# Batch 0's second 256 tokens by seven half-size products, w_out's first quarter ahead of w_in's last, and a new order of all steps

## The chip, the cores and the metric

The kernel runs on one core of a Trainium2 chip. The metric is the device time of one execution in microseconds. The core's engines run side by side, each in the order of its own program: TensorE (PE: matrix products), VectorE (DVE), ScalarE (ACT) and GpSimd (POOL: elementwise work; POOL here also issues the loads), and SyncE (SP: stores and transposes by DMA). They wait for each other by semaphores only.

## The reference

Cross attention between tokens and a small state, per batch and head, then two matrix products with a PReLU between:

```python
scores = scale * np.matmul(x, state.transpose(0, 1, 3, 2))     # B, H, S, D = 8, 8, 512, 64; 32 states
a = np.exp(scores - scores.max(-1, keepdims=True))
a /= a.sum(-1, keepdims=True) + 1e-09
xread = np.matmul(a, state)                                    # 512 rows per batch
scores2 = scale * np.matmul(state, x.transpose(0, 1, 3, 2))    # its softmax is a2
sread = np.matmul(a2, x)                                       # 32 rows per batch
x = concatenate([xread, sread])                                # 4352 rows of 512, heads side by side
h = x @ w_in                                                   # 512 x 2048
g = np.maximum(h, 0.0) + alpha * np.minimum(h, 0.0)
out = g @ w_out                                                # 2048 x 512
```

## The kernel before

Products are in float16, sums in float32. The work is cut by batch: batches 0 to 7 are 512 token rows each; "batch 8" is the 256 state reads of all batches together. The function has one method for each step, and a table of tokens, `ORDER` (lines 17 to 136), says in which order the steps are called; that order is each engine's program order. A token has the step's name, its indices, the engine where there is a choice (a ScalarE, v VectorE, p GpSimd), and the PSUM bank or buffer. There are eight banks of 128x512 float32; a product into a bank waits until the last reader of the bank is done.

The steps that matter here:

- `lx`, `wi`, `wo` (lines 199 to 262): loads of a batch's x, of a quarter of w_in (512 hidden columns) and of a quarter of w_out (512 hidden rows). GpSimd issues them all, and they land in the order of issue.
- Attention weights of tokens: `sc` scores on TensorE, `sb` a 32x32 transpose on VectorE (L466), `smax` (VectorE, L476), `ssh` (GpSimd, L482), `sexp` (ScalarE, L488), `ssum` (VectorE, L492, L493), `snorm` (GpSimd, L496), `wb` the transpose back on VectorE (L504). After `wb` of a batch its weights, aT, are ready. For the states: `tm` (L514), `tms`, `te` (ScalarE, L519, L527), `tsum` (L537), a DMA transpose, `rd` state reads (L553), `rn` (L565).
- `m` (L590): the states of a batch times a quarter of w_in; `mo` (L603) casts the two halves from PSUM. So a hidden row comes from the weights and `m`, without xread.
- `F` (L620), for a batch and one of 16 blocks of 128 hidden columns: two products of 512 columns, needing `wb` and `mo`; `f` (L641) is half of one. `N` (ScalarE, L652) writes the negative part, `G` (VectorE, L656) the PReLU of it, called prelude below, which also frees the bank.
- The second product in full size, `S` (L675): for 128 tokens, two of 16 blocks at a time, 512 columns; `O` (L719) copies the sum out. Eight `S` for 128 tokens.
- The second product of 256 tokens in seven half-size products in place of eight. The 2x2 blocks are: two quarters of 128 tokens, two halves of the hidden rows, two halves of 256 output columns. `W` (L745) makes four sums of w_out blocks, once for all batches, in two parts each. `A` (L765) makes the four sums of hidden blocks, two parts each. `P` (L793) is one of the seven products, in two parts of four matrix products of 256 columns: 14 `P` for 256 tokens. `C` (L805) copies a partial result out of the bank that is still added to, four times, and `D` (L810) adds the other banks to three of them. `st` stores 128 rows.
- `Z` (L272): products of zeros, in units of 128 columns, on TensorE at the start.

The two methods that the change calls more often read so:

```python
def hidden_sum(b, i, s, f, e, k):
    qa, qb = quarters(b, i)
    ...
        1: (block(b, qb, f), block(b, qb, f + 2)),
        2: (hc.get((b, i, 1, f)), block(b, qa, f)),
        3: (block(b, qa, f), block(b, qb, f)),
        4: (block(b, qa, f + 2), hc.get((b, i, 2, f))),
```
```python
            rows = {
                ...
                5: lambda: hc[b, i, 1, hf][:, j, :],
            ...
            cols = {
                ...
                5: lambda: wc[1][:, jc, :],
```

The seven-product form is used for both halves of batches 1 to 7 and for batch 8. Batch 0 is done in full size: 32 `S`, four `O`.

Of the kernel before, what the change touches and what calls it, by code (L numbers as in the profile page):

```python
# [22 lines left out]
mo.2.0.a.1.2 mo.2.0.a.0 Z.4.5 xt.1.1.0.5 xt.1.0.0.5 xo2.1.0.v xt.1.1.1.6 xt.1.0.1.6 xo2.1.1.v
f.0.2.0.4 f.0.2.1 N.0.2.0 G.0.2 F.0.3.7 N.0.3.1 G.0.3 m.3.0.1.2 mo.3.0.a.1.3 mo.3.0.a.0 Z.5.4
m.0.1.0.3 mo.0.1.a.1.4 wo.3 mo.0.1.a.0 lx.2 sc.1.2.5.6 tm.1 f.0.0.0.4 f.0.0.1 N.0.0.2 sb.1 f.0.1.0.2
f.0.1.1 N.0.1.3 G.0.1 tms.1 m.4.0.7.1 mo.4.0.a.0.5 te.1.0 te.1.1 m.0.2.0.3 mo.0.2.v.0.6 m.1.1.7.2
mo.1.1.a.1.7 mo.4.0.a.1 mo.1.1.a.0 mo.0.2.v.1 smax.1 lx.3 ssh.p.1 W.1.0.p W.1.1.p G.0.0 F.0.5.0
F.0.7.5 m.1.3.6.3 mo.1.3.a.0.8 mo.1.3.v.1 F.0.4.2 N.0.4.0 G.0.4 N.0.7.1 G.0.7 N.0.5.3 F.0.10.1
F.0.6.7 tsum.0 F.0.8.6 N.0.8.2 G.0.8 G.0.5 m.0.3.4.3 N.0.10.0 G.0.10 mo.0.3.a.0.9 mo.0.3.a.1
S.0.1.0.2 S.0.1.1 S.0.2.0.5 S.0.2.1 m.2.1.6.4 mo.2.1.v.0.10 sexp.1 ssum.1 snorm.p.1 N.0.6.1 G.0.6  # L30
m.1.2.0.3 mo.1.2.a.1.11 mo.1.2.a.0 S.0.2.2 F.0.9.1 S.0.1.2 F.0.13.6 N.0.9.2 G.0.9 N.0.13.3 G.0.13
F.0.11.3 N.0.11.0 G.0.11 S.0.0.0.0 S.0.0.1 S.0.0.2 wb.1 F.0.15.7 F.0.12.1 S.0.1.3 N.0.15.1 G.0.15
F.0.14.6 N.0.14.2 G.0.14 S.0.2.3 S.0.1.4 S.0.0.3 N.0.12.3 G.0.12 mo.2.1.a.1 F.1.5.3 N.1.5.0 G.1.5
F.1.12.7 N.1.12.1 G.1.12 F.1.0.4 N.1.0.2 G.1.0 F.1.1.6 F.1.3.1 N.1.3.3 G.1.3 S.0.2.4 F.1.4.3 N.1.4.0
G.1.4 F.1.8.7 N.1.8.1 G.1.8 S.0.1.5 S.0.2.5 N.1.1.2 G.1.1 F.1.2.4 N.1.2.3 G.1.2 F.1.15.1 N.1.15.0
G.1.15 S.0.1.6 S.0.1.7 O.0.1.a.0 F.1.10.3 N.1.10.1 G.1.10 S.0.2.6 S.0.0.4 xd.2 sc.2.2.6.7 sb.2 tm.2
m.4.2.2.4 mo.4.2.a.0.12 smax.2 S.0.2.7 O.0.2.a.1 mo.4.2.a.1 S.0.3.0.1 F.1.9.3 N.1.9.2 G.1.9 tsum.1
F.1.11.2 N.1.11.3 G.1.11 W.0.0.p W.2.1.p W.0.1.p W.2.0.p W.3.1.p W.3.0.p A.1.0.3.0.p.0 A.1.1.3.0.p.1
tms.2 te.2.1 F.1.6.5 N.1.6.0 G.1.6 S.0.3.1 S.0.3.2 F.1.7.4 S.0.0.5 te.2.0 N.1.7.1 G.1.7 S.0.0.6
S.0.0.7 O.0.0.a.2 tt.0 tt.1 rd.0.3 rd.1.6 rn.1 A.1.1.1.0.v.0 A.1.0.3.1.v.0 m.2.3.7.2 mo.2.3.a.0.13  # L40
mo.2.3.a.1 xd.3 st.0.2 st.0.1 tt.2 S.0.3.3 F.1.13.5 ssh.p.2 sexp.2 N.1.13.2 m.3.1.0.4 mo.3.1.a.1.1
mo.3.1.a.0 A.1.1.2.0.p.0 rn.0 sc.3.2.6.7 tm.3 tms.3 lx.4 A.1.0.1.0.p.1 ssum.2 snorm.p.2 S.0.3.4
P.1.1.1.0.2 F.1.14.3 P.1.1.1.1 G.1.13 N.1.14.3 G.1.14 A.1.1.1.1.p.0 S.0.3.5 S.0.3.6 P.1.0.2.0.4
P.1.0.1.0.0 S.0.3.7 te.3.0 te.3.1 tt.3 sb.3 P.1.1.2.0.5 P.1.1.2.1 C.1.1.1.a.3 D.1.1.0 P.1.0.1.1
O.0.3.a.1 st.0.3 st.0.0 tsum.2 wb.2 m.2.2.3.1 mo.2.2.a.1.4 mo.2.2.a.0 m.3.2.6.7 mo.3.2.a.0.6 rd.2.5
lx.5 xd.4 A.1.1.2.1.p.0 P.1.0.2.1 mo.3.2.a.1 rt.0.1 rdo.0.a rn.2 smax.3 P.1.1.6.0 A.1.0.2.0.v.1
A.1.0.4.0.p.0 F.2.7.3 N.2.7.0 G.2.7 F.2.1.5 N.2.1.1 G.2.1 C.1.0.1.a.0 D.1.0.0 F.2.8.6 N.2.8.2 G.2.8
F.2.2.7 F.2.3.1 N.2.2.3 N.2.3.0 G.2.2 P.1.0.6.0 F.2.5.3 N.2.5.1 P.1.1.6.1 F.2.0.5 N.2.0.2 G.2.5
G.2.3 P.1.0.5.0.4 C.1.1.2.a F.2.11.6 N.2.11.3 G.2.11 G.2.0 A.1.0.1.1.p.1 P.1.0.5.1 F.2.9.7 P.1.1.7.0
F.2.10.3 N.2.10.1 xd.5 G.2.10 F.2.4.1 N.2.9.0 G.2.9 F.2.14.6 N.2.4.3 G.2.4 N.2.14.2 G.2.14  # L50
A.1.1.3.1.p.1 A.1.0.2.1.p.1 P.1.0.6.1 C.1.0.2.a P.1.1.7.1 ssh.p.3 sexp.3 ssum.3 P.1.1.5.0.5 F.2.13.3
rt.2.7 rdo.2.a P.1.0.7.0 C.1.1.3.a.1 P.1.0.7.1 C.1.0.3.a.2 D.1.0.1 F.2.12.1 N.2.12.1 F.2.6.6
P.1.1.5.1 G.2.12 N.2.6.0 F.2.15.7 N.2.15.3 A.1.0.4.1.p.0 G.2.6 G.2.15 N.2.13.2 G.2.13 P.1.0.4.0
P.1.0.4.1 A.2.0.1.0.p.1 C.1.0.4.a A.1.1.4.0.p.1 P.1.0.3.0 A.2.1.3.0.p.1 P.1.0.3.1 D.1.0.2 st.1.0
D.1.1.1 P.1.1.4.0 P.1.1.4.1 C.1.1.4.a st.1.3 tsum.3 rd.3.6 rn.3 sc.4.2.0.1 snorm.p.3 wb.3 m.3.3.7.3
m.4.1.4.2 mo.4.1.a.0.9 mo.3.3.a.1.0 mo.3.3.a.0 A.1.1.4.1.p.1 A.2.0.2.0.p.1 P.1.1.3.0 mo.4.1.a.1
A.2.1.1.0.v.0 A.2.0.4.0.v.0 P.2.0.1.0.6 P.2.0.1.1 P.2.0.2.0.4 C.2.0.1.a.0 F.3.5.3 N.3.5.1
A.2.0.1.1.v.1 A.2.0.2.1.p.1 F.3.1.7 N.3.1.0 tm.4 tms.4 P.2.0.6.0 P.2.0.2.1 D.2.0.0 G.3.5 F.3.3.2
# [804 lines left out]
```

## Time and profile before

| what | value |
|---|---|
| median of three runs | 208.69 us (207.89 to 210.45) |
| the profiled execution's own time | 207.22 us |
| its span, first to last instruction | 205.4 us |
| granted TensorE clock | 1.000 |
| TensorE idle before 25 us, and from 25 to 200 us | 4.6 us, 0.25 us |
| x of batch 1 lands | 14.3 us |

Every time in the profile is in microseconds from the span's start unless marked ns. A row of the timeline has start, length, engine, line, operation, output and inputs, the count of instructions merged in it, and in brackets the idle time before them with what ended it. Consecutive instructions of an engine overlap a little at their ends, so the length of a row over its count is closer to an instruction's price than the mean of one.

### The profile page before, as it was taken

The page shows a single profiled execution, that of the slowest core. Times are in us where ns is not written, and L with a number is a line of the kernel's source. Part 1 is how long each engine was busy: PE and PEld are TensorE (multiplying, and loading weights), DVE is VectorE, ACT ScalarE, POOL GpSimd, SP SyncE. Part 2 cuts the span into 40 slices and gives each one's busy share as a digit, 9 for nine tenths or more (in the row PEclk, how much of TensorE's full clock was granted, in tenths as well). Part 3 has the DMA queues.
Part 4 walks back from the last instruction along what each step waited for, and adds up shares of the span by engine and source line. Part 5 has one row for each costly group of instructions (what it writes and reads, how often), then busy time and mean ns, then how long its engine had stood idle before and what let it go on. Part 6 is the DMA issues. An engine that isn't in the chain of part 4 may idle for free.

```text
span 205.4 us, 5181 instructions
## 1 busy us (share of the span) xinstructions
PE 197.1 (96%) x2023; PEld 131.4 (64%) x2023; DVE 181.6 (88%) x321; ACT 145.2 (71%) x319; POOL 159.6 (78%) x136
## 2 busy tenths in 40 slices
PE   7887999999999999999999999999999999999993
PEld 2542344445757766766557776776778777788882
DVE  4799999999999989999899999989999699995841
ACT  2599997889897679899898878869666476411120
POOL 7575489999989979998998899987997988502220
PEclk9999999999999999999999999999999999999999
DMA  5999999995999342749990135022000220031124
GB/s 81 195 203 209 204 206 197 185 232 54 163 163 178 66 153 58 100 103 158 194 163 3 53 123 135 3 105 102 0 0 3 111 93 3 2 131 62 69 102 156
DMA packets 39257, 23.22 MB, mean 113 GB/s; under 512 B 22320, under 2 KB 35008, under 8 KB 39232
## 3 DMA queue, kind: packets, MB, share of 16 engines
q0 software_dynamic: 12704, 8.59, 29.3%
q1 hardware_dynamic: 26496, 14.29, 28.4%
q8 instruction: 16, 0.26, 0.6%
q14 instruction: 9, 0.07, 0.2%
q10 hardware_dynamic: 32, 0.01, 0.0%
HBM read 17.31 MB, written 8.91 MB: 128 GB/s over the span
## 4 chain that ended last, share of the span: by engine, by line
PE 85%; DVE 5%; DMA 5%; POOL 1%; ACT 1%; issue 1%; ACTq 0%; POOLq 0%
PE ps L793 44%; PE ps L620 24%; PE ps L675 7%; DMA xg<-in_x_dram 5%; PE ps L629 3%; PE ps L590 3%; DVE gt_all L656 3%; PE ps L553 1%; ACT neg_all L652 1%; PE ps L362 1%; DVE m_all L603 1%; POOL xg L218 1%; DVE ts L466 1%; DVE nb L514 1%; DVE mx L476 1%
## 5 line engine op out<-in xcount | busy, mean ns | idle before, releaser
L656 DVE SCALAR_TENSOR_TENSOR gt_all<-neg_all,oma_sb,ps 128x512 f16<-128x512 f32 x128 | 89.3, 738 | 3.0 <-ACT neg_all L652 2.7
L652 ACT ACTIVATE neg_all<-ps 128x512 f32<-128x512 f32 (+1 forms) x144 | 77.4, 598 | 20.0 <-PE ps L620 14.4
L620 PE MATMUL ps<-aT,m_all 128*128 128x512 f16 x250 | 66.4, 379 | 0.3 <-DVE m_all L603 0.2
L765 POOL TENSOR_TENSOR hc_all<-gt_all 128x512 f16<-128x512 f16 x43 | 49.2, 1160 | 11.4 <-DVE osb_all L810 8.7
L793 PEld LDWEIGHTS <-hc_all 128*128 128x128 f16 x480 | 46.3, 98 | 14.3 <-issue 1.1
L793 PE MATMUL ps<-wc,hc_all 128*128 128x256 f16 x360 | 47.7, 273 | 0.0
L793 PEld LDWEIGHTS <-gt_all 128*128 128x128 f16 x336 | 32.6, 98 | 8.3 <-issue 0.5
L805 ACT COPY osb_all<-ps 128x256 f32<-128x256 f32 x51 | 19.1, 383 | 25.7 <-PE ps L793 22.2
L620 PEld LDWEIGHTS <-m_all 128*128 128x128 f16 x250 | 24.0, 98 | 18.0 <-issue 2.2
L603 ACT CAST m_all<-ps 128x512 f16<-128x512 f32 x58 | 31.6, 621 | 4.3 <-PE ps L590 4.3
L765 POOL TENSOR_TENSOR hc_all<-gt_all,hc_all 128x512 f16<-128x512 f16 x22 | 25.4, 1164 | 6.3 <-DVE hc_all L765 6.1
L793 PE MATMUL ps<-w_out_sb,gt_all 128*128 128x256 f16 x224 | 29.7, 273 | 0.0
L765 POOL TENSOR_TENSOR hc_all<-hc_all,gt_all 128x512 f16<-128x512 f16 x21 | 24.3, 1164 | 3.9 <-DVE hc_all L765 3.6
L810 DVE TENSOR_TENSOR osb_all<-osb_all,ps 128x256 f32<-128x256 f32 x45 | 18.0, 413 | 7.6 <-PE ps L793 4.7
L496 POOL TENSOR_TENSOR an<-ts,r 128x1024 f16<-128x1024 f32 (+1 forms) x9 | 15.5, 1725 | 6.2 <-DVE r L493 4.0
L482 POOL TENSOR_TENSOR ts<-ts,mx 128x1024 f32<-128x1024 f32 x7 | 13.4, 1918 | 5.4 <-DVE mx L476 5.4
L675 PE MATMUL ps<-w_out_sb,gt_all 128*128 128x512 f16 x64 | 16.6, 380 | 0.1
L793 PE MATMUL ps<-w_out_sb,hc_all 128*128 128x256 f16 x120 | 16.5, 273 | 0.0
L793 PE MATMUL ps<-wc,gt_all 128*128 128x256 f16 x112 | 14.7, 273 | 0.0
L590 PE MATMUL ps<-w_in_sb,stT 64*32 64x512 f16 x256 | 11.8, 383 | 1.9 <-DMA w_in_sb<-in_moe_w_in_dram 0.9
L527 ACT ACTIVATE e<-ps,nb 128x512 f16<-128x512 f32 x16 | 11.1, 705 | 0.1
L675 PEld LDWEIGHTS <-gt_all 128*128 128x128 f16 x64 | 5.9, 98 | 7.2 <-issue 1.2
(78 smaller groups left out, 204.6 us busy)
## 6 DMA issues: line engine op xcount, KB each, us to landing
out_dram<-osb_all SPq DMA_DIRECT2D x33, 256.0 KB, 2.6
xg<-in_x_dram POOLq DMA_DIRECT2D x7, 512.0 KB, 9.1
w_in_sb<-in_moe_w_in_dram POOLq DMA_DIRECT2D x4, 512.0 KB, 12.0
w_out_sb<-in_moe_w_out_dram POOLq DMA_DIRECT2D x4, 512.0 KB, 13.6
xg<-in_x_dram POOLq DMA_DIRECT2D x2, 256.0 KB, 4.5
out_dram<-osb_all SPq DMA_DIRECT2D x2, 128.0 KB, 2.4
gs_all<-in_state_dram POOLq DMA_DIRECT2D x1, 192.0 KB, 6.8
st<-in_state_dram SPq DMA_DIRECT2D x1, 128.0 KB, 2.4
```

Of the source, the lines that this page charges most:

```text
L482: engine(e).tensor_tensor(ts, ts, over_blocks(cols(softmax_tile("mx", b), j, S // N)), ALU.subtract)
L496: engine(e).tensor_tensor(blocks(cols(softmax_tile("an", b), j, S)), blocks(cols(softmax_tile("ts", b), j, S)), over_blocks(cols(softmax_t ...
L590: nc.tensor.matmul(banks[N * k : N * (k + 1), (k0, k1)[g], :], st_head(b, 2 * k + g)[64 * g : 64 * g + 64, :], w_in_sb[64 * g : 64 * g + 6 ...
L603: copier(e)(ms[b, f][:, g, :], banks[:, live["mp", b, f][g], :])
L620: nc.tensor.matmul(h.rearrange("p (r t) -> p r t", r=2), ms[b, f][:, g, 128 * j : 128 * (j + 1)], weights(b, g), start=(g == 0), stop=(g = ...
L652: nc.scalar.activation(neg, h, RELU, bias=0.0, scale=-1.0)
L656: nc.vector.scalar_tensor_tensor(gts[b, f][:, j, :], negs.pop((b, jc)), oma_sb[:, jc : jc + 1], hs.pop((b, jc)), ALU.mult, ALU.add,)
L675: nc.tensor.matmul(outs[b, q], hidden(b, jc, q), w_out_sb[:, jc, :], start=(jc == 0), stop=(jc == n_jc - 1),)
L765: engine(e).tensor_tensor(t, x, y, ALU.add if s == 1 else ALU.subtract)
L793: nc.tensor.matmul(outs[b, i, bank], rows, cols, start=(p in (1, 2, 5) and jc == 0), stop=(jc == n_jc // 2 - 1), skip_group_check=True,)
L805: copier(e)(rows_at(b, q, k)[:, 256 * half : 256 * (half + 1)], outs[b, i, "x"])
L810: nc.vector.tensor_tensor(to, to, outs[b, i, bank], ALU.add)
```

## The change

Only the table `ORDER` differs; it has two lines more, so line numbers behind it are higher by two (L656 becomes L658). The methods are the same.

```diff
-lx0.0 lx0.1 id ni.v wi.0 oma lst stc Z.7.32 stt.2 sto.a lx.1 wi.1 dd.0.0.v wi.2 Z.7.3 xt.0.0.0.6
+lx0.0 lx0.1 id ni.v wi.0 stc Z.1.22 stt.3 lst sto.a dd.0.0.v oma lx.1 wi.1 Z.1.10 xt.0.0.0.2
```

- Tokens 256 to 511 of batch 0 (quarters 2 and 3): 16 `S` and two `O` go; 14 `P`, eight `A` (six on GpSimd, two on VectorE), four `C` and three `D` come. Tokens 0 to 255 stay in full size.
- The loads are issued in the order w_in 0, 1, 2, w_out 0, w_in 3, w_out 1, 3, 2 in place of w_in 0 to 3, w_out 0 to 3.
- One part of one weight sum (`W`) moves to VectorE. Over the whole kernel 13 more `A` stand on GpSimd and five fewer on VectorE; VectorE has four more `C`, three more `D` and two fewer `mo`. Units of zeros: 73 before, 47 now.
- All steps get new places and banks.

VectorE, from the copies of batch 1's transposed x (L348, now L350) to the state maximum of batch 1 (L476, now L478). L656/L658 is the prelude, L603/L605 the cast of `m`, L514 and L466 the reductions and transposes of the scores. Before:

```order
L348 COPY xT_336<-ps 128x4x256 x2
L656 SCALAR_TENSOR_TENSOR gt_all<-neg_all,oma_sb,ps 128x512 x2
L514 TENSOR_REDUCE nb_395<-ps 128x2
L466 STREAM_TRANSPOSE ts_400<-ps 128x1024
L656 SCALAR_TENSOR_TENSOR gt_all<-neg_all,oma_sb,ps 128x512
L603 CAST m_all<-ps 128x512 x2
L476 TENSOR_REDUCE mx_441<-ts_400 128x32
```

And now:

```order
L350 COPY xT_332<-ps 128x4x256 x2
L658 SCALAR_TENSOR_TENSOR gt_all<-neg_all,oma_sb,ps 128x512
L468 STREAM_TRANSPOSE ts_377<-ps 128x1024
L516 TENSOR_REDUCE nb_394<-ps 128x2
L478 TENSOR_REDUCE mx_404<-ts_377 128x32
```

Two preludes and two casts less stand ahead of the maximum.

VectorE again, from there to the transpose that ends batch 1's weights (L504, now L506). Before:

```order
L476 TENSOR_REDUCE mx_441<-ts_400 128x32
L656 SCALAR_TENSOR_TENSOR gt_all<-neg_all,oma_sb,ps 128x512
L603 CAST m_all<-ps 128x512
L656 SCALAR_TENSOR_TENSOR gt_all<-neg_all,oma_sb,ps 128x512 x2
L537 RECIPROCAL r_0_308<-r_0_308 128x2
L656 SCALAR_TENSOR_TENSOR gt_all<-neg_all,oma_sb,ps 128x512 x3
L603 CAST m_all<-ps 128x512
L492 TENSOR_REDUCE r_1_511<-ts_400 128x32
L493 RECIPROCAL r_1_511<-r_1_511 128x32
L656 SCALAR_TENSOR_TENSOR gt_all<-neg_all,oma_sb,ps 128x512 x4
L504 STREAM_TRANSPOSE aT_550<-an_514 128x1024
```

And now:

```order
L478 TENSOR_REDUCE mx_404<-ts_377 128x32
L658 SCALAR_TENSOR_TENSOR gt_all<-neg_all,oma_sb,ps 128x512 x2
L605 CAST m_all<-ps 128x512
L658 SCALAR_TENSOR_TENSOR gt_all<-neg_all,oma_sb,ps 128x512 x2
L494 TENSOR_REDUCE r_1_428<-ts_377 128x32
L495 RECIPROCAL r_1_428<-r_1_428 128x32
L605 CAST m_all<-ps 128x512 x2
L658 SCALAR_TENSOR_TENSOR gt_all<-neg_all,oma_sb,ps 128x512 x3
L506 STREAM_TRANSPOSE aT_492<-an_431 128x1024
```

Three preludes and a reciprocal (moved ahead of the copies of x) less, one cast more.

GpSimd, from the loads of w_in's later quarters to the row sums of batch 0 (L765, now L767; wc is a weight sum, L745, now L747; an the norm, ts the shift). Before:

```order
L253 DMA w_in_sb<-in_moe_w_in_dram 128x4x512 x3
L496 TENSOR_TENSOR an_298<-ts_240,r_0_242 128x512 x2
L259 DMA w_out_sb<-in_moe_w_out_dram 128x4x512 x4
L201 DMA xg_377<-in_x_dram 128x8x256
L201 DMA xg_443<-in_x_dram 128x8x256
L482 TENSOR_TENSOR ts_400<-ts_400,mx_441 128x1024
L745 TENSOR_TENSOR wc_446<-w_out_sb 128x1024 x2
L496 TENSOR_TENSOR an_514<-ts_400,r_1_511 128x1024
L745 TENSOR_TENSOR wc_676<-w_out_sb 128x1024
```

And now:

```order
L255 DMA w_in_sb<-in_moe_w_in_dram 128x4x512 x2
L261 DMA w_out_sb<-in_moe_w_out_dram 128x4x512
L498 TENSOR_TENSOR an_246<-ts_240,r_0_242 128x512 x2
L255 DMA w_in_sb<-in_moe_w_in_dram 128x4x512
L261 DMA w_out_sb<-in_moe_w_out_dram 128x4x512 x3
L203 DMA xg_344<-in_x_dram 128x8x256
L203 DMA xg_397<-in_x_dram 128x8x256
L484 TENSOR_TENSOR ts_377<-ts_377,mx_404 128x1024
L747 TENSOR_TENSOR wc_419<-w_out_sb 128x1024
L767 TENSOR_TENSOR hc_all<-gt_all 128x512
L498 TENSOR_TENSOR an_431<-ts_377,r_1_428 128x1024
L747 TENSOR_TENSOR wc_419<-w_out_sb 128x1024
```

Two loads have changed places, and row sums of batch 0 stand between the weight sums.

VectorE's steps between two such transposes (`wb`), counted from the order; what is not in the table is the same:

| stretch | | preludes | row sums `A` | sums `D` | weight sums | norms `rn` | state maxima | `tsum` |
|---|---|---|---|---|---|---|---|---|
| batch 1 to batch 3 | before | 35 | 3 | 5 | 0 | 4 | 2 | 3 |
| | now | 38 | 7 | 8 | 1 | 3 | 2 | 3 |
| batch 3 to batch 4 | before | 14 | 3 | 7 | 0 | 0 | 2 | 0 |
| | now | 15 | 2 | 6 | 0 | 2 | 1 | 1 |

TensorE's steps left from the first `F` of a batch on: of batch 3, 96 `F` and 180 `P` before, 96 and 181 now, with one `rd` more; of batch 4, 80 `F`, 149 `P` before, 81 and 153 now, with one `rd` less.

More of the change, by code (lines that the diff above doesn't have):

```diff
@@ L23 @@
[L23 to L58, printed above, removed]
@@ new lines @@
+P.6.0.7.1 C.6.0.3.v.3 G.7.6 P.8.0.1.0.6 P.8.0.1.1 P.6.0.4.0 C.8.0.1.v.2 A.8.0.1.0.p.0 P.8.0.5.0.3
+P.6.0.5.1 D.6.0.1 P.6.1.3.1 D.6.1.2 D.6.0.0 st.6.2 A.8.0.1.1.p.0 A.8.0.2.1.v.0 P.7.1.1.0.2
+A.7.0.1.0.v.1 A.8.0.2.0.p.0 P.7.1.1.1 P.6.0.3.0 A.7.1.1.0.v.0 A.7.0.2.0.v.1 P.8.0.6.0 P.6.0.4.1
+C.6.0.4.a st.6.1 F.7.12.4 N.7.12.1 P.8.0.5.1 P.8.0.6.1 A.6.0.4.1.v.0 G.7.12 A.8.0.4.0.v.1
+A.8.0.3.1.v.1 C.7.1.1.a.1 A.7.0.3.0.p.0 C.8.0.2.a A.8.0.3.0.p.1 A.7.0.3.1.p.0 P.7.0.5.0.0
+P.7.0.1.0.1 P.6.0.3.1 P.7.1.2.0.4 P.8.0.7.0 P.8.0.7.1 A.7.0.1.1.v.1 A.7.1.1.1.v.0 D.6.0.2
@@ L136 @@
+A.7.0.4.1.p.1 P.7.0.3.0 P.7.0.3.1 D.7.0.2 st.7.0 P.7.0.4.0 P.7.0.4.1 C.7.0.4.a sv.7.1.0
 """
```

193 lines of the change are left out of this document (112 added, 81 removed).

## The prediction

> **What bounds the kernel now.** I read the page's shares first, then its 40 slices, then busy time by stage, then the orders of time of Vector, Scalar and TensorE where stages meet, then the chain of waits.
>
> ```profile
> span 205.4 us, 5181 instructions
> PE 197.1 (96%) x2023; PEld 131.4 (64%) x2023; DVE 181.6 (88%) x321; ACT 145.2 (71%) x319; POOL 159.6 (78%) x136
> PE   7887999999999999999999999999999999999993
> DVE  4799999999999989999899999989999699995841
> ```
>
> TensorE is full from the fifth slice to the last, and Vector is nearly as full up to the thirty-third. The stages below are cut where Vector ends batch 0's and then batch 1's, 3's and 4's attention weights (first column start and end, then length, then busy time of each engine).
>
> ```profile
> 16.35:33.61 17.26, 15.66 (x142) 6.17 (x135) 17.07 (x26) 15.96 (x35) 11.53 (x8) 1.00 1.28 205
> 33.61:73.44 39.83, 39.83 (x454) 23.41 (x453) 39.16 (x64) 33.41 (x73) 38.33 (x28) 1.00 0.90 152
> 73.44:96.33 22.89, 22.89 (x223) 15.69 (x221) 22.22 (x34) 20.88 (x49) 21.26 (x18) 1.00 0.56 106
> 96.33:201.90 105.57, 105.40 (x1016) 79.60 (x1014) 91.52 (x175) 65.40 (x148) 76.78 (x65) 1.00 0.29 76
> ```
>
> Up to 33.61 us Vector is busy for 17.07 of 17.26 and TensorE is not: Vector sets the pace. Up to 73.44 both are full: TensorE 39.83, Vector 39.16 of 39.83. Only after 96.33 has Vector 14 us to spare. How tightly the two are coupled shows where a batch's weights end (L504 on Vector) and its first hidden product begins (L620 on TensorE):
>
> ```profile
> 15.07 1.29 DVE L348 COPY xT<-ps 128x1024 f16<-128x1024 f16 x2 [0.32 <-PE ps L340]
> ...
> 32.37 1.24 DVE L504 STREAM_TRANSPOSE aT<-an 128x1024 f16<-128x1024 f16 x1
> ...
> 72.20 1.24 DVE L504 STREAM_TRANSPOSE aT<-an 128x1024 f16<-128x1024 f16 x1
> ...
> 93.97 1.21 DVE L476 TENSOR_REDUCE mx<-ts 128x32 f32<-128x1024 f32 x1
> 95.10 1.24 DVE L504 STREAM_TRANSPOSE aT<-an 128x1024 f16<-128x1024 f16 x1
> ```
> ```profile
> 34.03 1.24 PE L620 MATMUL ps<-aT,m_all 128*128 128x512 f16 x5
> ...
> 73.99 1.03 PE L620 MATMUL ps<-aT,m_all 128*128 128x512 f16 x4
> ...
> 96.92 1.03 PE L620 MATMUL ps<-aT,m_all 128*128 128x512 f16 x4
> ```
>
> Batch 1's weights end at 33.61 and its products begin at 34.03; batch 3's at 73.44 and 73.99; batch 4's at 96.33 and 96.92. TensorE takes them just in time, so work added to Vector ahead of these points delays TensorE, and TensorE, whose order is fixed and which has no idle time later, can't win it back. The end is TensorE's last product at 201.9 and a fixed tail:
>
> ```profile
> 28.15 0.43 PE ps L620 x2
> 28.58 0.43 PE ps L675 x2
> ...
> 195.98 5.91 PE ps L793 x54
> ...
> 201.91 0.37 ACT osb_all L805
> ```
>
> **What the change removes on TensorE.** 16 steps S go, 32 products of 512 columns at 0.43/2 = 0.215 us: 6.9 us. 14 steps P come, 56 products of 256 columns at 5.91/54 = 0.109: 6.1. TensorE saves 0.8 us. The copies on Scalar (two of 512 columns against four of 256) stay about level. This saving counts only where TensorE sets the end.
>
> **What it adds ahead of 73.44 us.** The prices per instruction, Vector's first, then Scalar's, then GpSimd's:
>
> ```profile
> 20.75 1.28 DVE L603 CAST m_all<-ps 128x512 f16<-128x512 f32 x2
> ...
> 25.64 0.16 DVE L537 RECIPROCAL r<-r 128x2 f32<-128x2 f32 x1
> ...
> 29.83 2.62 DVE L656 SCALAR_TENSOR_TENSOR gt_all<-neg_all,oma_sb,ps 128x512 f16<-128x512 f32 x4
> ...
> 48.14 0.28 DVE L565 TENSOR_TENSOR sn<-ps,r 128x128 f16<-128x128 f32 x1
> 48.34 0.87 DVE L765 TENSOR_TENSOR hc_all<-gt_all 128x512 f16<-128x512 f16 x2
> ...
> 71.08 0.74 DVE L810 TENSOR_TENSOR osb_all<-osb_all,ps 128x256 f32<-128x256 f32 x2
> ```
> ```profile
> 14.07 0.24 ACT L527 ACTIVATION_READ_ACCUMULATOR e<-ps,nb 128x1 f32 x1
> ...
> 20.30 0.75 ACT L527 ACTIVATE e<-ps,nb 128x512 f16<-128x512 f32 x1
> ...
> 21.64 2.10 ACT L603 CAST m_all<-ps 128x512 f16<-128x512 f32 x4
> 23.54 2.65 ACT L652 ACTIVATE neg_all<-ps 128x512 f32<-128x512 f32 x5
> ...
> 26.88 1.23 ACT L488 ACTIVATE ts<-ts 128x1024 f32<-128x1024 f32 x1
> ```
> ```profile
> L765 POOL TENSOR_TENSOR hc_all<-gt_all x43: 1146/1157/1272, 44.4 to 188.5; 128x512 f16<-128x512 f16 x43
> ...
> L745 POOL TENSOR_TENSOR wc<-w_out_sb x4: 2118/2130/2143, 25.1 to 36.1; 128x1024 f16<-128x1024 f16 x4
> ```
>
> First stretch, from xT of batch 1 (ready at 16.36, since x of batch 1 is loaded in the same place) to batch 1's weights. Vector now has five preludes of L656 fewer ahead of them (5 x 0.655 = 3.3), one cast fewer (0.64), one small reciprocal fewer (0.16): 4.1 us less, so by Vector alone the weights end at 33.6 - 4.1 = 29.5. But Scalar must pass 13 casts and 8 negatives at 0.53, two exponentials (20.30 to 21.64, 1.34), a shift (about 0.25) and the state exponential (26.88 to 27.84 where the next begins, 0.96) between the end of batch 0's exponentials (14.31) and the negative that the last prelude needs: 13.7 us. Also the second token shift now stands behind the product on w_in's first quarter, which puts its exponential about 0.6 later (an estimate: it ran while Scalar waited for that product). That is 28.6, then a prelude and the transpose, 1.9: 30.5. Scalar's bound is the later, so I take 30.4, 3.2 earlier than now; the two sums, 29.5 and 31.0 with a wait between, are the ends.
>
> Second stretch, from batch 1's weights to batch 3's. By the counts in the table Vector gets three preludes (2.0), four row sums of L765 (4 x 0.435 = 1.7), three sums of L810 (1.1) and one weight sum of twice a row sum's width, which Vector has never done here: between one row sum, 0.4, and what GpSimd needs for it, 2.1; nearest is two row sums, 0.9. One normalising goes (-0.3). Together 5.4 us: 39.83 + 5.4 = 45.2, and batch 3's weights end at 30.4 + 45.2 = 75.6 instead of 73.44. Vector's 0.67 us of idle time may swallow some of it; the long weight sum may add 1.2.
>
> From there TensorE. Batch 3's first product comes 0.55 later, at 76.15 instead of 73.99: 2.2 late. What is left for TensorE then is one P (0.44) and one step of state reads (32 small products, 0.3 as an estimate, less than a P) more than before: 2.9 in all. The same sum at batch 4: Vector's stretch loses 0.6 (one prelude and the normalisings more, one maximum and two sums fewer), so its product begins at 75.6 + 22.3 + 0.6 = 98.5 against 96.92, 1.6 late, with 1.9 more left (one F, four P, less a read): 3.5 at most, and 2.2 if the 0.67 idle in each stretch is used. I take **2.8 us slower**, with 1.0 and 4.5 as ends.
>
> The last rows of TensorE's order are of the same kind as before, so the tail is kept. The profiled run is 207.22 us for a span of 205.4, hence 210.0 as such; it lies 1.47 below the median of 208.69. Median predicted: 208.69 + 2.8 = **211.5 us**.
>
> **What I cost at nothing.**
>
> ```profile
> 13.45 3.04 POOL L259 DMA_DIRECT2D w_out_sb<-in_moe_w_out_dram  x4
> ...
> 23.24 1.91 POOL L482 TENSOR_TENSOR ts<-ts,mx 128x1024 f32<-128x1024 f32 x1 [5.00 <-DVE mx L476]
> 25.12 4.21 POOL L745 TENSOR_TENSOR wc<-w_out_sb 128x1024 f16<-128x1024 f16 x2
> ```
> ```profile
> w_out_sb<-in_moe_w_out_dram POOLq DMA_DIRECT2D x1, 512.0 KB, 11.0
> ```
>
> The exchange of two loads: w_out's first quarter was issued at 13.45 and landed 11.0 later, at 24.45. It takes w_in's place about 2 us earlier, and w_in's last quarter gets the 24.45. Its first product now stands behind a cast of Scalar that lies five steps ahead of the 28.6 above, near 26.0, which covers the landing. All other loads behind keep their slots. On GpSimd the issues move past nothing long.
>
> The eight new row sums, six on GpSimd: the state maximum now stands behind two preludes and two casts fewer (2.6), so it ends near 20.6 and the state shift near 22.6. From there to the sum that P.0.1.5.1 needs GpSimd passes seven weight sums (14.9), four row sums (4.6) and a norm (1.9): 44.0. TensorE's first product of batch 1 waits for the bank of the second prelude behind the transpose, 31.9, and P.0.1.5.1 lies 13.1 us of products behind that, near 45. So it is covered by 1 us; each us beyond is one lost.
>
> **A rule against the change.** The longest row sum of Vector beside a GpSimd sum took 0.54 (the pair at 48.34 took 0.87 together), and GpSimd's longest 1.27 against 1.16. The Trainium skill, SBUF — State Buffer, § SBUF: two separate sides, says that a Vector instruction with two SBUF inputs and a GpSimd one exclude each other for the whole instruction. By it the weight sum on Vector would wait out up to 2.1 us and each Vector row sum up to 1.2; the rows show about 0.1, so I leave it out of the sum.
>
> **Rivals.**
> 1. Not slower: Vector isn't the bound. If batch 1's weights end by 28 or Vector's added sums fall in gaps, TensorE's 0.8 us shows: 207.9. For it: TensorE is 96% busy, Vector 88% over the whole. Against it: 17.07 of 17.26 and 39.16 of 39.83.
> 2. Slower by far: GpSimd's row sums come late for P.0.1.5.1. W of w_out's third quarter waits for the load issued last; if GpSimd ends 2.6 us later than 44.0, the 1.0 of cover is gone and 1.6 come on top: 213.1, and over 2% from 2.3 us on.
> 3. A cold TensorE. The first fillers (below) took 0.45 each, 0.215 later; the change drops 26 of 73 units of filler, most between 11.9 and 17 us. If TensorE falls back there, some 3.4 us of products take double: 1.7 more, 213.2. Against it: it still gets real work at least every 2 us there. The Trainium skill, TensorE: Matmul & The Clock Gate, § Part 1, puts the fall behind a whole window of idleness of about 3.4 us; no row shows a fall.
> 4. The lock of SBUF, as a mechanism: one Vector weight sum held 2.1 and two row sums 1.2 each: 4.5 more at worst, 2.1 in the mean, 213.6.
>
> ```profile
> 1.32 3.60 PE L272 MATMUL ps<-gs_all 128*128 128x512 f16 x8 [1.32 <-DVE gs_all L266]
> ```
>
> **How the numbers follow.** Slower by 1.0 to 4.5 around 211.5: 0.53. Rival 1: 0.22; rival 2: 0.13; rivals 3 and 4: 0.04 each; faster than any of them: 0.04. About 2%, or 4.2 us, is what a measurement of this kernel can tell from no change: below 204.5 or above 212.9. Faster: 0.03. Slower: of the first case 0.07, of rival 2 0.10, of 3 and 4 0.05: 0.22. Within: 0.75. The range leaves out half of rival 1 below and the far half of rival 2 above: 208.1 to 214.0.
>
> **What would show it.** Batch 1's transposed weights ending near 30.4, batch 3's near 75.6, with Vector idle for under 1 us between; TensorE idle for some tenths at a time between 30 and 75, waiting for copies and preludes, and full after 98. It would be wrong if batch 3's weights end by 73.5, or if TensorE waits for GpSimd near 45, or for w_in at 24.5.

## The result, and the profile after

| | before | changed |
|---|---|---|
| median of 4 executions | 208.64 us (207.89 to 210.45) | 211.21 us (210.09 to 212.00) |
| ratio to before | | 1.0139 [1.0095, 1.0184] |
| profiled execution, its span | 207.22 us, 205.4 us | 210.09 us, 208.1 us |

The changed kernel is slower by 2.6 us, 1.4%; the interval of its ratio lies above 1, but 1.4% is inside the 2% that count as no difference here. A ratio leaves out executions more than 1.5% above the fastest of their kernel, a median takes all. The forecast was 211.5 us, 2.8 slower. The number came out; the sum behind it did not, as the views show one by one.

First the page of the changed kernel: its span, its shares and the slices of TensorE.

```profile
span 208.1 us, 5223 instructions
PE 196.4 (94%) x2039; PEld 132.8 (64%) x2039; DVE 181.8 (87%) x322; ACT 145.6 (70%) x319; POOL 171.9 (83%) x148
PE   7867899999999999999999999999999999999981
```

TensorE is busy for 0.7 us less than before, and the span is 2.7 us longer: 3.4 us more of idleness. That 0.7 is not the forecast's 0.8: the products of zeros alone are busy for 4.7 us in place of 6.8 (13 products in place of 21), so the rest of TensorE's work is not less by this view. The last digit but one tells where some of it lies: 8, where the row of before had a 9. Next the same four stages as in the prediction, cut anew where batch 1's, 3's and 4's weights end (start and end, length, busy time of each engine, clock, DMA).

```profile
16.36:29.53 13.17, 10.91 (x105) 3.87 (x104) 13.13 (x19) 13.17 (x29) 10.94 (x8) 1.00 1.23 203
29.53:73.58 44.05, 43.99 (x470) 26.81 (x469) 43.70 (x73) 37.08 (x80) 41.33 (x31) 1.00 0.87 143
73.58:95.96 22.38, 22.38 (x277) 15.44 (x277) 21.60 (x35) 19.98 (x46) 20.65 (x18) 1.00 0.58 119
95.96:203.60 107.64, 106.96 (x1000) 80.75 (x997) 92.51 (x172) 65.00 (x146) 87.42 (x75) 1.00 0.29 76
```

The first stage is 4.1 us shorter, the second 4.2 longer, the third 0.5 shorter, the last 2.1 longer. In the last one TensorE, which had 0.17 us of idleness in 105.57 before, has 0.68 in 107.64. The two ends of the second stage in the order of time of Vector, and where batch 3's and batch 4's products begin on TensorE:

```profile
28.29 1.24 DVE L506 STREAM_TRANSPOSE aT<-an 128x1024 f16<-128x1024 f16 x1
...
72.36 1.22 DVE L506 STREAM_TRANSPOSE aT<-an 128x1024 f16<-128x1024 f16 x1
```
```profile
74.36 0.59 PE L622 MATMUL ps<-aT,m_all 128*128 128x512 f16 x2
...
96.25 1.03 PE L622 MATMUL ps<-aT,m_all 128*128 128x512 f16 x4
```

Batch 3's weights end at 73.58 (before 73.44, forecast 75.6); its first product starts at 74.36 (before 73.99, forecast 76.15). So TensorE begins batch 3 only 0.37 us late, with the 0.7 us of added steps still ahead of it: 1.1 of the span's 2.7. Batch 4 says the same: its first product starts at 96.25, 0.7 earlier than before (96.92, forecast 98.5), with the forecast's 1.9 us more of steps ahead of it, 1.2 in all. In between Vector and TensorE are close to a tie. The chain of waits of the changed kernel runs through Vector's preludes up to 45 us and through TensorE's products from 46.6 on; before, it was TensorE's alone there.

```profile
29.53 13.21 DVE gt_all L658 x20
...
47.04 0.98 PE ps L795 x8
```

The rest is at the end. The chain of waits there, with start and length of each piece:

```profile
196.55 0.43 DVE osb_all L812
...
197.00 3.75 DMA out_dram<-osb_all
...
200.85 0.38 ACT osb_all L807
...
201.25 0.43 DVE osb_all L812
...
201.72 1.92 PE ps L795 x16
...
203.67 0.37 ACT osb_all L807
```

Before, this chain was TensorE alone to 201.9. Now a store stands in it. Batch 8's finished rows leave row buffer 2 from 197.00 on; the copy C.7.0.3.a.2 on Scalar needs that buffer, starts at 200.85, and behind it stand the sum D.7.0.1 on Vector and then P.7.0.3.0, which waits for the bank. TensorE's own row gives its idle time in the brackets. SyncE's rows of the changed kernel and of the kernel before show what follows: the stores of the last rows (L724 and L722 whole rows, L728 and L726 half rows).

```profile
201.72 1.03 PE L795 MATMUL ps<-w_out_sb,hc_all 128*128 128x256 f16 x8 [0.63 <-DVE osb_all L812]
```
```profile
202.13 1.45 SPq L724 DMA_DIRECT2D out_dram<-osb_all  x3
204.07 0.33 SPq L728 DMA_DIRECT2D out_dram<-osb_all  x1
```
```profile
200.62 1.20 SPq L722 DMA_DIRECT2D out_dram<-osb_all  x2
202.31 0.33 SPq L726 DMA_DIRECT2D out_dram<-osb_all  x1
```

From the issue of the last half row to the end of the span it takes 208.1 - 204.07 = 4.0 us; before it was 205.4 - 202.31 = 3.1. Three whole rows stand close ahead of it now, where there were two. The profiled executions of the runs below mostly bear this out: with three whole rows issued in some 1.45 us the tail is 3.8 to 4.0 us in four traces, with three in 1.86 us it is 3.3, and with two in 1.0 to 1.2 us it is 3.1 to 3.2. Two traces with the stores further apart do not fit, at 3.5 and 3.7 us. So the trace puts 0.6 us of waiting and 0.9 of tail on the end, 1.5 together, which the forecast had at nothing.

### The profile page after: what moved, and what is told of

Read it like the earlier page. It is cut to its first block, busy times and chain, and to the rows that moved or that the text cites. A ratio compares the mean times of both kernels' runs of the same rounds, so it can differ in the third digit from the quotient of the medians.

```text
span 208.1 us, 5223 instructions
## 1 busy us (share of the span) xinstructions
PE 196.4 (94%) x2039; PEld 132.8 (64%) x2039; DVE 181.8 (87%) x322; ACT 145.6 (70%) x319; POOL 171.9 (83%) x148
## 3 DMA queue, kind: packets, MB, share of 16 engines
q0 software_dynamic: 12704, 8.59, 28.6%
## 4 chain that ended last, share of the span: by engine, by line
PE 73%; DVE 14%; DMA 6%; POOL 1%; issue 1%; ACT 1%; ACTq 0%; POOLq 0%
PE ps L795 44%; PE ps L622 20%; DVE gt_all L658 9%; DMA xg<-in_x_dram 5%; PE ps L631 3%; PE ps L592 3%; DMA out_dram<-osb_all 2%; PE ps L555 1%; DVE ts L468 1%; DVE m_all L605 1%; ACT e L529 1%; DVE xT L350 1%; PE ps L364 1%; POOL xg L220 1%; DVE nb L516 1%
## 5 line engine op out<-in xcount | busy, mean ns | idle before, releaser
L658 DVE SCALAR_TENSOR_TENSOR gt_all<-neg_all,oma_sb,ps 128x512 f16<-128x512 f32 x128 | 88.7, 739 | 4.7 <-ACT neg_all L654 4.3
L767 POOL TENSOR_TENSOR hc_all<-gt_all 128x512 f16<-128x512 f16 x50 | 57.2, 1158 | 6.9 <-PE ps L795 6.4
L795 PEld LDWEIGHTS <-hc_all 128*128 128x128 f16 x512 | 49.4, 98 | 15.1 <-issue 2.5
L795 PE MATMUL ps<-wc,hc_all 128*128 128x256 f16 x384 | 50.5, 273 | 0.0
L795 PEld LDWEIGHTS <-gt_all 128*128 128x128 f16 x360 | 34.6, 98 | 9.4 <-issue 1.5
L605 ACT CAST m_all<-ps 128x512 f16<-128x512 f32 x60 | 33.0, 610 | 3.3 <-PE ps L592 3.3
L767 POOL TENSOR_TENSOR hc_all<-gt_all,hc_all 128x512 f16<-128x512 f16 x26 | 30.0, 1166 | 3.2 <-DVE hc_all L767 2.3
L795 PE MATMUL ps<-w_out_sb,gt_all 128*128 128x256 f16 x240 | 32.5, 273 | 0.0
L767 POOL TENSOR_TENSOR hc_all<-hc_all,gt_all 128x512 f16<-128x512 f16 x21 | 24.2, 1158 | 6.6 <-DVE hc_all L767 6.4
L795 PE MATMUL ps<-w_out_sb,hc_all 128*128 128x256 f16 x128 | 18.1, 273 | 0.6 <-DVE osb_all L812 0.6
L592 PEld LDWEIGHTS <-stT 64*32 64x32 f16 x256 | 3.8, 89 | 11.3 <-issue 7.4
L516 DVE TENSOR_REDUCE nb<-ps 128x2 f32<-128x1024 f32 x8 | 9.6, 1204 | 0.7 <-PE ps L364 0.6
```

What stands on the lines that cost most here:

```text
L592: nc.tensor.matmul(banks[N * k : N * (k + 1), (k0, k1)[g], :], st_head(b, 2 * k + g)[64 * g : 64 * g + 64, :], w_in_sb[64 * g : 64 * g + 6 ...
L605: copier(e)(ms[b, f][:, g, :], banks[:, live["mp", b, f][g], :])
L658: nc.vector.scalar_tensor_tensor(gts[b, f][:, j, :], negs.pop((b, jc)), oma_sb[:, jc : jc + 1], hs.pop((b, jc)), ALU.mult, ALU.add,)
L767: engine(e).tensor_tensor(t, x, y, ALU.add if s == 1 else ALU.subtract)
L795: nc.tensor.matmul(outs[b, i, bank], rows, cols, start=(p in (1, 2, 5) and jc == 0), stop=(jc == n_jc // 2 - 1), skip_group_check=True,)
```

## The experiments

Each comparison gives the ratio to the kernel before, run beside it on the same chip. The kernel before had 60 executions in all there, in three sets with medians of 208.19, 208.14 and 208.15 us. Since one rival is a cold TensorE, the granted clock that each execution shows is told where it matters; an execution "whose clock did not fall" is one with a mean of 0.995 or more.

### The end: a fifth row buffer

The one copy that waits goes to another buffer, a slot of the negatives that nothing reads any more.

```diff
     def rows_at(b, q, i):
         if i is not None:
-            osbs[b, q] = osb_all[:, i]
+            osbs[b, q] = osb_all[:, i] if i < 4 else neg_all[:, 2]
...
-C.7.0.3.a.2
+C.7.0.3.a.4
```

> The changed kernel with one edit: the output rows of tokens 128 to 255 of batch 7 go to a fifth row buffer (a slot of neg_all that nothing reads any more), so that their copy at 200.85 us need not wait 4.96 us for the store of batch 8's rows. Theory E (what the prediction left at nothing: some 1.6 us of the loss lie in the last 12 us, 0.7 as TensorE waiting behind that copy and 0.95 as a longer tail of the last store): TensorE's last product ends 0.6 to 0.8 us earlier, the whole comes 0.7 us (if the three whole-row stores still stand bunched before the last one) to 1.6 us earlier, 209.6 to 210.5 us. Theory V (the prediction's: Vector's added steps between batch 1's and batch 3's weights cost it all, the end is kept): 211.2 us, no change over 0.3.

Measured: 211.07 us, ratio 1.0111 [1.0058, 1.0164]. By the medians alone this is unclear. The profiled execution shows the mechanism itself: TensorE passes the place without a pause.

```profile
200.61 1.03 PE L790 MATMUL ps<-wc,gt_all 128*128 128x256 f16 x8
201.48 1.91 PE L790 MATMUL ps<-w_out_sb,hc_all 128*128 128x256 f16 x16
```
```profile
202.34 1.86 SPq L719 DMA_DIRECT2D out_dram<-osb_all  x3
204.69 0.33 SPq L723 DMA_DIRECT2D out_dram<-neg_all  x1
```

Its span is 208.0 with the last half row issued at 204.69, a tail of 3.3 us. But five of its six executions had a granted clock of 0.974 to 0.991; the one at 1.000 took 208.68 us. The fifth buffer in the kernel before is the control:

```diff
-            osbs[b, q] = osb_all[:, i]
+            osbs[b, q] = osb_all[:, i] if i < 4 else neg_all[:, 1]
...
-C.7.0.1.a.2
+C.7.0.1.a.4
```

> The kernel before with a fifth row buffer for the one copy that waits for a store there (1.67 us, at 190.85 us, while TensorE goes on). Both theories: 208.6 us within 0.3, since TensorE does not stand behind that copy; it is the control to the first run, and would show whether a fifth buffer by itself changes the time.

Measured: 209.09 us, 1.0027 [0.9996, 1.0057], no gain: a buffer is worth something only where TensorE stands behind the copy.

### The clock: zero products put back

```diff
-m.4.0.4.1
+Z.4.8 m.4.0.4.1
...
-F.0.3.2
+F.0.3.2 Z.1.4
```

> The changed kernel with 12 units of zero products put back where TensorE waits early on: 8 ahead of the product that waits for the states' copies (11.4 to 13.2 us in its trace), 4 ahead of the one that waits for w_in (18.3 to 19.3 us). Theory C (cold): in the runs of the changed kernel above their best the granted clock falls to 0.5 for some 3 us near 23.6 us, as the profile of the run with the fifth buffer shows (0.81, 0.50, 0.84 in 22 to 28 us after TensorE was busy 2.0 of 4 us); so mean clocks come to 0.996 or more, from 0.987 to 0.992, and the time to 209.6 to 210.3 us, from 211.2. Against it (places and end alone): clocks and time stay, 211.2 us within 0.4.

Measured: 210.21 us, 1.0093 [1.0059, 1.0127], five of eight executions at 0.998 to 1.000 and three at 0.992. The same with the fifth buffer:

```diff
-            osbs[b, q] = osb_all[:, i]
+            osbs[b, q] = osb_all[:, i] if i < 4 else neg_all[:, 2]
...
-m.4.0.4.1
+Z.4.8 m.4.0.4.1
...
-F.0.3.2
+F.0.3.2 Z.1.4
...
-C.7.0.3.a.2
+C.7.0.3.a.4
```

> Both repairs of the changed kernel: the 12 units of zero products and the fifth row buffer. If cold stretches and the end are the whole loss: 208.3 to 209.0 us, the kernel before within 0.4%. If Vector's added steps cost some 2 us of their own, as the prediction had it: 210 us or more.

Measured: 209.65 us, 1.0044 [1.0016, 1.0072], seven of twelve executions at 0.996 to 1.000. Between these two stands one edit, the buffer. By executions whose clock did not fall it takes 210.10 us without the buffer (median of five) and 208.62 with it (of seven), 1.5 us. Two of those seven, at 209.89 and 210.04 us, do not show it; by the ratios, and by the executions whose clock did fall (211.15 and 210.14), it is 1.0. So the end is worth 1.0 to 1.5 us, where the trace said 1.5.

The changed kernel once more, unaltered:

> The changed kernel unaltered, on the chip of the next three runs, to have its clocks and times in more executions beside the repaired versions: 211.2 us within 0.5, most clocks at 0.987 to 0.997. If it stands at 210.2 us or less, the 1 us that the 12 units of zero products seemed to bring was only the chip or chance.

Measured: 210.75 us, 1.0120 [1.0075, 1.0166], three of six executions at 0.998 to 1.000 and three at 0.979 to 0.992. It is not below 210.2, but its interval overlaps that of the zero products, so that their 1 us is not shown. What the profiled execution (0.992) shows is where the clock goes. Busy time by stretches of 2 us, the granted clock standing behind the five engines' busy times; then TensorE's order of time:

```profile
18.00:20.00 2.00, 1.08 (x12) 0.22 (x10) 2.00 (x3) 2.00 (x7) 0.49 (x1) 1.00 1.24 206
20.00:22.00 2.00, 0.99 (x17) 0.40 (x17) 2.00 (x4) 2.00 (x7) 1.47 (x1) 1.00 1.24 207
22.00:24.00 2.00, 1.97 (x18) 0.70 (x11) 2.00 (x4) 2.00 (x4) 1.60 (x2) 0.51 1.25 206
24.00:26.00 2.00, 2.00 (x7) 0.56 (x5) 1.97 (x4) 1.96 (x4) 2.00 (x2) 0.63 1.25 208
```
```profile
19.22 0.41 PE L592 MATMUL ps<-w_in_sb,stT 64*32 64x512 f16 x8 [0.92 <-DMA w_in_sb<-in_moe_w_in_dram]
...
21.15 1.88 PE L592 MATMUL ps<-w_in_sb,stT 64*32 64x512 f16 x24 [0.98 <-DVE gt_all L658]
...
23.87 1.82 PE L677 MATMUL ps<-w_out_sb,gt_all 128*128 128x512 f16 x4
```

After 4 us in which TensorE worked for half the time, it runs at about half speed for some 3.4 us: four products of w_out take 1.82 us, in the first trace of the same kernel 1.02. That execution, at 0.997, took 210.09 us in all, this one 211.04. That is rival 3, which the prediction gave 0.04. But the idleness alone does not decide it: the first trace has the same of it, 2.06 us of work in the same 4 us, and its clock stayed full.

```profile
18.00:20.00 2.00, 1.06 (x12) 0.23 (x10) 2.00 (x3) 2.00 (x6) 0.38 (x1) 1.00 1.19 194
20.00:22.00 2.00, 1.00 (x18) 0.40 (x17) 2.00 (x4) 2.00 (x7) 1.39 (x1) 1.00 1.23 208
22.00:24.00 2.00, 1.69 (x26) 0.58 (x12) 2.00 (x4) 2.00 (x5) 2.00 (x2) 1.00 1.24 204
```

It meets the kernel before as well, less often: 18 of its 60 executions lie below 0.995, with a median of 209.1 us against 208.0 for the other 42. Of the changed kernel's ten, six do, with a median of 211.6 against 210.05. Whether the zero products that were taken out make the difference stays open: with twelve units back it was 8 of 20 executions, without them (the first run of the fifth buffer counted in) 11 of 16, and profiled executions of both sorts fall near 22 us. The twelve units are little for a test, three products of 512 columns. Two more runs do not settle it. The kernel before without 24 of its units:

```diff
-Z.3.2
...
-Z.4.17
+Z.4.4
...
-Z.4.5
...
-Z.5.4
```

> The kernel before with 24 of its 73 units of zero products taken out (13 of the 17 ahead of batch 0's first weights, and the 2, 5 and 4 about them), so about as many as the changed kernel has; nothing else. Theory C: the clock falls in most runs, to a mean of 0.985 to 0.992, and the time rises by 1 to 2 us, to 209.3 to 210.3. Against it: no product waits for a zero product, so 208.2 us within 0.3 and clocks as before.

Measured: 211.03 us, 1.0106 [1.0068, 1.0144], with clocks of 0.989 to 0.998, three of six at 0.995 or more. The time rose in these three too (210.95 to 211.65), so not by the clock that was expected to fall. The profiled execution ended batch 1's weights 1.3 us later than before, stood 1.1 us behind a store near 122 us and had a tail 1.0 us longer. Part of the late start can be seen: eight transposes of x took 1.06 us, in the kernel before 0.62, ahead of the first unit taken out and while the record shows a granted clock of 1.00.

```profile
8.35 1.06 PE L336 MATMUL ps<-ident,xg 128*128 128x128 f16 x8
```
```profile
6.93 0.62 PE L340 MATMUL ps<-ident,xg 128*128 128x128 f16 x8
```

So the clock that is listed for an execution can leave out a slow start. Why all six are slow is not explained. And the kernel before with three units more:

```diff
-m.4.0.7.1
+m.4.0.7.1 Z.3.3
```

> The kernel before with 3 units of zero products more, ahead of the product that waits for w_in at 18.8 to 19.3 us (0.65 us of work in 0.5 us of wait). About 12 of its 42 runs so far had a clock of 0.988 to 0.992 and some 1 us more than the rest. If the clock falls for want of work there: those runs get rare, median 207.9 to 208.1 us; otherwise 208.2 to 208.4, some 0.1 later by the added work.

Measured: 208.28 us, 0.9994 [0.9969, 1.0019], three of twelve executions below 0.995: nothing that can be told from before. Nor was the test as strong as the expectation has it: three units are one product of 384 columns, 0.34 us long in its row, and not 0.65 us of work.

### Vector: five added sums, early and late

```diff
+    def extra_vector():
+        nc.vector.tensor_tensor(
+            early[:, 2048:2560], w_in_sb[:, 0, :512], w_in_sb[:, 1, :512], ALU.subtract
+        )
...
-G.1.0
+G.1.0 Y
...
-G.1.15
+G.1.15 Y
...
-G.1.6
+G.1.6 Y
...
-D.1.1.0
+D.1.1.0 Y
...
-G.2.9
+G.2.9 Y
```

> The kernel before with five added sums of 128x512 on Vector that nothing reads (5 x 0.33 to 0.42 = 1.7 to 2.1 us), all between batch 1's and batch 3's weights, where the prediction had Vector set the time. The prediction's rule: what Vector gets there comes out at the end, 209.9 to 210.3 us. By what the trace of the changed kernel showed (that stretch took 44.05 us with 2.9 us more of Vector's work forecast, and batch 3 began 0.4 us late): 208.3 to 209.3 us, since Vector's order has slack that the products' order takes up.

Measured: 211.04 us, 1.0107 [1.0072, 1.0142]. The prediction's rule holds for the place: the stage between batch 1's and batch 3's weights takes 42.26 us in place of 39.83, and the profiled span grows by 1.8 us, the time by 2.2 (1.5 to 3.0 by the ratio and its interval). What the expectation missed is the price. The five took 3.6 us and not 2.1. The stage, and the group of the five (busy us, mean ns):

```profile
33.74:76.00 42.26, 41.29 (x457) 23.88 (x456) 41.91 (x69) 34.38 (x73) 38.79 (x28) 1.00 0.92 146
```
```profile
L702 DVE TENSOR_TENSOR gs_all<-w_in_sb 128x512 f16<-128x512 f16 x5 | 3.6, 717 | 0.0
```

The executions fall into two groups, about 209.3 (four) and 211.4 us (eight), and the profiled one belongs to the first. Of the second group five show a clock of 0.991 or 0.992 and three one of 0.997 to 1.000; what it loses beyond the first was not seen. The control has the same five late, with their unread result in m_all:

```diff
-            early[:, 2048:2560], w_in_sb[:, 0, :512], w_in_sb[:, 1, :512], ALU.subtract
+            m_all[:, 12, 0, :], w_in_sb[:, 0, :512], w_in_sb[:, 1, :512], ALU.subtract
...
-G.1.0 Y
+G.1.0
...
-G.7.0
+G.7.0 Y
...
-G.7.5
+G.7.5 Y
...
-G.7.8
+G.7.8 Y
...
-G.7.9
+G.7.9 Y
...
-G.7.14
+G.7.14 Y
```

> The kernel before with the same five added sums on Vector as before, now at 163 to 175 us, among batch 7's preludes, where TensorE has a long order ahead: 208.2 to 208.6 us if only Vector's work ahead of batch 3's weights comes out at the end, as the prediction's rule says (the five early ones made batch 3's weights 2.4 us later and the profiled span 1.8 us longer). If any work on Vector costs its time: 210 us.

Measured: 209.96 us, 1.0088 [1.0054, 1.0123], and the expectation fails: late work on Vector costs too, 1.8 us (1.1 to 2.6), not clearly less than early work. TensorE waited 0.8 and 0.4 us there for preludes. The five took 4.2 us, and the orders of time of Vector and of GpSimd say why:

```profile
165.24 1.17 DVE L702 TENSOR_TENSOR m_all<-w_in_sb 128x512 f16<-128x512 f16 x1
...
172.29 0.41 DVE L702 TENSOR_TENSOR m_all<-w_in_sb 128x512 f16<-128x512 f16 x1
...
175.45 1.12 DVE L702 TENSOR_TENSOR m_all<-w_in_sb 128x512 f16<-128x512 f16 x1
```
```profile
175.14 1.16 POOL L766 TENSOR_TENSOR hc_all<-gt_all,hc_all 128x512 f16<-128x512 f16 x1
176.25 1.34 POOL L766 TENSOR_TENSOR hc_all<-gt_all 128x512 f16<-128x512 f16 x1
```

At 172.29 GpSimd has no sum under way, and Vector's takes 0.41. At 175.45 GpSimd is in its sum of 175.14, which ends at 176.30; Vector's ends at 176.57, 0.27 behind it, and GpSimd's next, begun at 176.25, takes 1.34 in place of 1.16. The two take turns. This is rival 4's mechanism, seen.

### The seven products themselves

The changed kernel, batch 0's second half at full width again: the A, C and D steps of batch 0 go, and the fourteen P become sixteen S at the same places.

```diff
-P.0.1.1.0.3
+S.0.2.0.3
...
-P.0.1.5.0.5
+S.0.3.0.5
...
-P.0.1.3.1
+S.0.3.7 O.0.3.a.3 st.0.3
```

> The changed kernel with batch 0's second 256 tokens again in eight full-width products, everything else at its new places: 5 steps fewer on Vector (some 2.0 us), 6 fewer on GpSimd (7.1 us), TensorE 32 x 0.215 = 6.9 in place of 56 x 0.109 = 6.1 us. Theory V: Vector set the second stretch, so batch 3's weights come about 2 us earlier and the whole about 2 us, 208.5 to 209.5 us. Theory E: only some 1.1 us of the loss stand at batch 3's start, TensorE gets 0.8 us more work, the end's 1.6 us stay: 210.3 to 211.2 us. A third, that the new places and not the seven products cost the time: 211.2 to 212.0 us.

Measured: 213.35 us, 1.0198 [1.0138, 1.0257]. By the ratio that is 212.3 us (211.1 to 213.5), above every theory's range, though its interval reaches into the third's. The profiled execution took 215.74 us with a mean clock of 0.973, so that only its inner stage is read, where the clock was full. From batch 1's to batch 3's weights TensorE was busy for 45.4 us of 46.8, against 43.99 of 44.05 in the changed kernel, and it waited 1.4 us for an exponential behind a copy of 512 columns that this edit put ahead of it. So the run does not price the seven products cleanly. It does show that taking some 2 us from Vector gave nothing there: Vector now had 4.1 us to spare in the stage (42.65 of 46.79), and TensorE, with 1.4 us more of work and that wait, set its length.

### The exchange of the two loads

The exchange alone, in the kernel before:

```diff
-wi.3
...
-snorm.p.0.0
+wo.0 snorm.p.0.0
...
-snorm.p.0.1
+snorm.p.0.1 wi.3
...
-wo.0
```

> The kernel before with the exchange of loads alone: the first quarter of w_out where the last quarter of w_in stood, that quarter of w_in behind batch 0's last weights, all else as it was. The prediction put the exchange at nothing: 208.6 us within 0.3, since the first product that reads the last quarter comes late enough. Against it: if a product of batch 0 or 1 now waits for that quarter, TensorE starts later by that wait, and 0.5 to 1.5 us are added.

Measured: 211.78 us, 1.0164 [1.0120, 1.0208]. TensorE stands for 3.0 us, and the clock falls with it (0.68 from 24 to 26 us, 0.50 in the next 4; the mean is 0.983 to 0.992 in all six executions), so the 3.4 us of the ratio are not the wait alone. The wait:

```profile
26.71 0.63 PE L586 MATMUL ps<-w_in_sb,stT 64*32 64x512 f16 x8 [3.02 <-DMA w_in_sb<-in_moe_w_in_dram]
```

And the new places with the old order of the loads:

```diff
-wo.0
+wi.3
...
-wi.3
+wo.0
```

> The changed kernel with the two loads exchanged back (w_in's last quarter ahead, w_out's first behind batch 0's last weights), all else as changed: the other half of the run that had the exchange alone in the old places, which came out 3 us longer with TensorE waiting 3.0 us for w_in's last quarter. The first product of w_out's first quarter starts at 23.80 us here, GpSimd's first weight sum at 22.48. If each order of loads only suits its own places: w_out's quarter lands about 25 to 27 us, TensorE waits 1.5 to 3 us for it, 212.5 to 214 us. If the exchange is idle in the new places: 211.2 us within 0.4.

Measured: 211.60 us, 1.0165 [1.0126, 1.0205]; its four executions at 0.996 or more took 211.05 to 211.80, the changed kernel's four such 209.99 to 210.46. The other quarter is late now:

```profile
25.00 1.04 PE L672 MATMUL ps<-w_out_sb,gt_all 128*128 128x512 f16 x4 [1.04 <-DMA w_out_sb<-in_moe_w_out_dram]
```

So each order of the loads belongs to its own places of the products. No version here beats the kernel before; the best of the changed kind, with both repairs, is 0.4% behind it.

## Why the prediction was right in number and wrong in its sum

By executions whose clock did not fall, the change costs 210.05 - 207.99 = 2.1 us. The fifth buffer takes back 1.0 to 1.5 of that, so 0.6 to 1.1 is left for Vector and the moved steps, where the trace reads 1.1. The two traces differ by more, 210.09 - 207.22 = 2.9 us, because the kernel before was profiled in an execution 0.8 below its 207.99; so what is read from them against each other is rather too much. The medians over all executions differ by 2.6, and the 0.5 between goes with the clock, which fell more often.

- **First stretch, "so I take 30.4".** Batch 1's weights ended at 29.53, where Vector's own sum (29.5) had them. Scalar did not hold them up, though only just: the negative that the last prelude needs was written at 27.52, and Vector came to that prelude at 27.63, where the forecast had 28.6 for the first. I had priced its casts and negatives at 0.53, a row's length by its count; but a row's length has the last instruction's tail in it, and these start closer together:

```profile
26.38 0.63 ACT L605 CAST m_all<-ps 128x512 f16<-128x512 f32 x1
26.85 0.67 ACT L654 ACTIVATE neg_all<-ps 128x512 f32<-128x512 f32 x1
27.34 0.66 ACT L605 CAST m_all<-ps 128x512 f16<-128x512 f32 x1
27.80 0.69 ACT L654 ACTIVATE neg_all<-ps 128x512 f32<-128x512 f32 x1
```

  Three steps in 1.42 us is 0.47 each; over 21 of them that is 1.2 us, more than the 0.9 by which the stretch was missed.
- **Second stretch, 45.2 us.** It took 44.05. The same fault: two row sums in a row took 0.75, so a further one costs 0.34 and not 0.435, and the weight sum 0.68 and not 0.87; that is 0.6 of the 1.15 us. Vector's idle time, which went from 0.67 to 0.35 us, is 0.3 more; the rest was not traced.

```profile
45.65 0.75 DVE L767 TENSOR_TENSOR hc_all<-hc_all,gt_all 128x512 f16<-128x512 f16 x2
...
47.64 0.68 DVE L747 TENSOR_TENSOR wc<-w_out_sb 128x1024 f16<-128x1024 f16 x1
```

- **"I take 2.8 us slower" from these two.** This is the mis-sized term: 0.37 us of delay at batch 3's first product and 0.7 of added steps, 1.1 in all; 0.6 to 1.1 by the experiments. The rule under it, that Vector's work ahead of batch 3's weights comes out at the end, was right by the five sums (2.6 us later at the weights, 1.8 at the end of the profiled span, and 1.3 by the first group's 209.3 against 207.99). That it is free later on was implied by "only after 96.33 has Vector 14 us to spare", and was wrong: spare time over a stage is not spare time at a place.
- **"The last rows of TensorE's order are of the same kind as before, so the tail is kept."** This step failed. The kinds were the same, but not which row buffer each copy reuses nor how the stores bunch: 1.5 us by the trace, 1.0 to 1.5 by the buffer's runs. The wait for the buffer is shown by taking it away; that the bunching makes the tail longer is read from the traces' tails alone. The two errors, 1.7 to 2.2 too much and 1.0 to 1.5 too little (and the clock's 0.5), cancelled: that the number came out is luck.
- **"It would be wrong if batch 3's weights end by 73.5."** They ended at 73.58, so this sign of being wrong was missed by 0.08 us. Of the signs of being right, Vector was idle for under 1 us (0.35), but TensorE was idle for 0.06 us in the second stage and not for some tenths at a time, and it was not full after 98: it waited 0.63 us at 201.1.
- **Rival 1, Vector is not the bound.** False as put (slower, not 207.9), but near: in the second stage TensorE was busy for 43.99 us of 44.05, Vector for 43.70, and in the run that took 2 us from Vector there TensorE set the stage's length.
- **Rival 2, GpSimd late for P.0.1.5.1.** It did not come. The sum before it stood in this row of GpSimd, the first of the two ending at 43.50 (forecast 44.0), and the product in this row of TensorE, at 44.67 (near 45):

```profile
42.34 2.27 POOL L767 TENSOR_TENSOR hc_all<-gt_all 128x512 f16<-128x512 f16 x2
```
```profile
44.23 1.04 PE L795 MATMUL ps<-wc,hc_all 128*128 128x256 f16 x8
```

- **Rival 3, a cold TensorE.** Real, in six of ten executions, and near its price of 1.7 us: 1.6 by the medians of the two sorts of executions, 1.0 in the pair of traces, 1.1 in the kernel before. My reason against it, real work at least every 2 us, does not protect it. That the zero products taken out bring it on is not shown.
- **Rival 4, the lock.** I read the wrong thing out of the rows. They showed 0.1 us because 27 of the 32 such sums of Vector in the kernel before stand where GpSimd has none under way, not because the two can overlap. The Trainium skill, SBUF — State Buffer, § SBUF: two separate sides, was right that the later one waits out the earlier, and the trace agrees: 0.41 us became 1.12 and 1.17. The longest of the rows, 0.54 us, was such a touch: begun at 48.34 inside GpSimd's shift, it ended 0.29 behind it. It cost little in the changed kernel, whose new places avoid it too (24 of 28 sums): the only touch of note is the weight sum of 47.64, for which GpSimd's shift took 2.29 us in place of 1.91.

- **The exchange of loads at nothing.** Right for the pair of exchange and places. Taken apart, either half loses: 3.0 us of waiting in the old places, 1.0 in the new.
- **Number and range.** 211.21 lies in 208.1 to 214.0.
